# Linear attention and a gated convolution layer on one core: q transposed on TensorE instead of by DMA, the rms factor spread by DMA for two groups instead of three, the convolution on TensorE for one batch instead of two

## The chip, the cores and the metric

The kernel runs on one core of a Trainium2 chip. The core has five engines that each work through their own instructions in order and wait for one another by semaphores: TensorE (PE, matrix products and transposes), VectorE (DVE), ScalarE (ACT), GpSimd (POOL) and SyncE (SP). Sixteen DMA engines move data between HBM and the on-chip memory SBUF. Matrix products land in PSUM, from which DVE or ACT must carry them on.

The metric is the device time of one execution in microseconds. The kernel before takes 247.41 us (median of three runs, 246.47 to 247.62). The execution that the profile shows spans 246.0 us and was timed at 247.78 us. Where an instant is given, it is counted from the start of that span.

## The reference

Eight batches, eight heads, 576 positions, 64 channels per head. First linear attention without softmax with a normalised output, then a layer with a convolution along the sequence as its gate:

```python
kv  = einsum('bhsd,bhse->bhde', k, v)            # 64 x 64 per head
out = einsum('bhsd,bhde->bhse', q, kv)
rms = sqrt(mean(out * out, axis=-1, keepdims=True) + 1e-06)
x   = out / rms * g_norm                         # heads side by side: (8, 576, 512)

h        = maximum(x @ w_in, 0)                  # 512 -> 1024
conv_out = sum of conv_w[k] * h shifted by k-1   # three taps along the sequence
y        = (h * sigmoid(conv_out)) @ w_out       # 1024 -> 512, float32 out
```

q, k, v and the weights come in float32; the DMA casts them to bf16 on the way in.

## The kernel before

The work is cut into five groups of batches, and a table per group says which of two ways is taken for each step. The number after the name of a group below is its place in these tables.

```python
BY_ACT = (1, 1, 1, 0, 0)      # 1/sqrt by ACT (Ln, Exp); 0: by Newton steps on POOL
Q_DMA  = (0, 0, 1, 1, 1)      # q transposed by DMA; 0: by PE
R_DMA  = (0, 0, 1, 1, 1)      # rms factor spread over partitions by DMA; 0: by PE
C_PE   = (1, 1, 0, 0, 0)      # convolution on PE; 0: on DVE
GROUPS = ((0,), (1,), (2, 3), (4, 5), (6, 7))
STEPS  = ((2, 2, 2, 2), (4, 4), (4, 4), (4, 4), (2, 2, 2, 1, 1))
```

Loads go out on POOL's queue, one for each of k, v and q of a batch. Two buffers exist for each name, so a load of batch b waits until the tile of batch b-2 has been read:

```python
loads = pool("loads", 2)
qkv[name, b] = loads.tile([PS, H, R * D], BF16, name=name + "_sb")
nc.gpsimd.dma_start(out=qkv[name, b][:, lo:hi, :], in_=src[b, lo:hi].rearrange(...))
```

q must lie with its channels on the partitions. The two ways (PE works in blocks of 96 positions by 128 channels, six blocks for each of four steps):

```python
if g.by_dma:                                    # Q_DMA
    def tr(...):
        g.qT[bi] = attn.tile([P, H, HS], BF16, name="qT", bufs=QT)
        nc.sync.dma_start_transpose(
            out=g.qT[bi].rearrange("c h (j p) -> c (h j) p", p=PS),
            in_=qkv["q", b].rearrange("p h m -> p (h m)"))
...
if not g.by_dma:
    def tr_mm(...):                             # four times a batch
        ps = one_bank([P, 2, HS], BF16, "qT_ps")
        for i in range(2):
            for j in range(J):
                nc.tensor.transpose(ps[:, i, j * PS:(j + 1) * PS],
                                    q_sb[:, 2 * t + i, j * P:(j + 1) * P], ident[:PS, :PS])
    def tr_out(...):
        move(tst["op"], g.qT[bi][:, 2 * t:2 * t + 2, :], tst["ps"])   # on DVE or ACT
```

For the normalisation, `product` computes `out` into PSUM (`ot_ps`, four small matmuls for a pair of heads), ACT squares it (`sq`), and PE sums the squares (`ss_ps`). ACT or POOL makes 1/sqrt of the sums (`rs`). Then, by R_DMA:

```python
if g.r_dma:                      # out is not kept, but computed a second time
    nc.sync.dma_start(out=scr, in_=g.rs)                   # to DRAM and back,
    for t in range(n_hd):                                  # copied to 64 partitions each
        for i in range(2):
            nc.sync.dma_start(out=g.rb[i * D:(i + 1) * D, t, :, :],
                              in_=row[i:i + 1].to_broadcast([D, 2 * g.G, HS]))
    st["ps"] = product(g, bi, t)                           # out_again
    nc.vector.scalar_tensor_tensor(g.xT[...], st["ps"], g_sb, g.rb[...], mult, mult)
else:                            # out is kept in SBUF (o32, DVE or ACT), rs cut into bf16
    move(ust["op"], g.o32[bi][:, t, :, :], ust["ps"][:, :, :HS], g_sb[:, 0:1])      # keep
    split()                                                # hi, low, mid, rsb on DVE
    nc.tensor.matmul(ps[:, i, :HS], spread[ts, 2 * bi + e, :], g.rsb[ts, :])        # rb_ps
    nc.vector.tensor_mul(g.xT[...], g.o32[bi][...], st["ps"][:, :, :HS])            # x_mul
```

The second half, per group: `h_ps` (eight matmuls for 128 of the 1024 columns and one batch), relu into `h` on ACT or DVE, the convolution, the sigmoid on ACT, the gate on DVE, and `o_ps` (eight matmuls for 128 positions), which ACT or DVE copies to `o_sb` for the store.

```python
if g.c_pe:       # convolution as matmuls with diagonal weights, eight per 128 columns
    nc.tensor.matmul(ps[:, e, off:off + n], diag[:, j, f, :], h[:, src:src + n], ...)    # c_ps
    nc.scalar.activation(cst["c"][...], st["ps"][:, :, :HS], AX.Sigmoid)
else:            # on DVE: two taps per 128 columns, two additions (three pieces) per step
    nc.vector.tensor_scalar_mul(cst["t"][...], g.h[:, f, :], cw_rel[:, j, f:f + 1])      # tap
    nc.vector.tensor_add(c[...], h[...], t[...])                                         # add
    nc.scalar.activation(cst["c"][...], cst["c"][...], AX.Sigmoid, scale=cw_rel[:, 1, f:f + 1])
...
nc.vector.tensor_mul(hs, hs, cst["c"])                                                   # gate
```

None of this is emitted in the order in which it is written. Each step is recorded as an operation with an engine, a cost in microseconds and the operations that it needs; `plan.order()` then plays the list through with these costs, tries 250 variations of the priorities, and emits the best order. Where an operation names two engines, the list also settles which of them does it. The order on each engine is thus fixed when the kernel is built, by costs that are written in the kernel:

```python
t_issue = plan.op("SP", 1.0, tr, deps=[loaded["q", b, h0]] + g.need_qT[bi])
tr_done = plan.op("XBAR", 9.0, None, deps=[t_issue])        # a transpose by DMA
i = plan.op("POOL", 1.3, load, b, name, src, deps=deps)
loaded[name, b, 0] = prev = plan.op("DMA", 3.1, None, deps=[i, prev])   # a load
sp = plan.op("BC", 4.0 + 2.5 * g.G, None, deps=[sc])        # the rms factor by DMA
land = plan.op("OUT", 0.0, None, deps=[so])                 # a store
```

The rings `TWO` (three double banks of PSUM, for `ot_ps`, `rb_ps`, `h_ps`, `c_ps`) and `ONE` (two banks, for `kv_ps`, `qT_ps`, `ss_ps`, `o_ps`) are part of that list too.

Of the kernel before, what the change touches and what calls it, by code (L numbers as in the profile page):

```python
# [54 lines left out]
FP32 = mybir.dt.float32  # L55
# [10 lines left out]
BY_ACT = (1, 1, 1, 0, 0)  # L66
Q_DMA = (0, 0, 1, 1, 1)
R_DMA = (0, 0, 1, 1, 1)
C_PE = (1, 1, 0, 0, 0)
NORM_TABLES = "natural_log_exp_and_others"  # L70
# [32 lines left out]
class Plan:  # L103
# [11 lines left out]
    def op(self, engines, cost, fn, *args, deps=()):  # L115
        engines = engines if isinstance(engines, tuple) else (engines,)
        o = Op(len(self.ops), engines, cost, fn, args, deps)
        o.group = self.group
        self.ops.append(o)
        return o  # L120

    def run(self, places, back=False):
# [13 lines left out]
        while events:  # L136
# [18 lines left out]
            for item in ready:  # L155
                o = ops[item[1]]
                e = next((e for e in o.engines if busy.get(e, 0.0) <= now + 1e-6), None)
                if e is None or not back and any(free[h.ring] < 1 for h in o.takes):
                    continue
                if not back:  # L160
                    for h in o.takes:
                        free[h.ring] -= 1
                end[o.at] = busy[e] = now + o.cost
# [21 lines left out]
    def order(self):  # L185
        ops = self.ops
        way = [0.0] * len(ops)
        for o in reversed(ops):
            way[o.at] = o.cost + self.HOP + max((way[u] for u in o.users), default=0.0)
        best = self.passes([-w for w in way], 8)  # L190
        rnd = random.Random(1)
        for _ in range(self.ROUNDS):
            width = rnd.choice((1, 2, 4, 8))
            each, shift = rnd.random() < 0.7, {}
            places = [e - o.cost + (rnd.gauss(0, width) if each else
                                    shift.setdefault((o.group, o.kind), rnd.gauss(0, width)))
                      for o, e in zip(ops, best[1])]
            got = self.passes(places, 2)
            if got[0] <= best[0]:
                best = got  # L200
        for o, e in zip(ops, best[2]):
            o.engine = e
        return [ops[i] for i in best[3]]


class Group:
    def __init__(self, n, bs, S):
        self.n, self.bs, self.G, self.T = n, bs, len(bs), S * len(bs)
        self.kv, self.qT, self.o32, self.sq = {}, {}, {}, {}
        self.n_o = 0  # L210
# [3 lines left out]
def kernel(  # L214
# [15 lines left out]
    P = 128  # L230
# [132 lines left out]
    def attention(g):  # L363

        first = g.n == 0
        sums = []
        for bi, b in enumerate(g.bs):
            kv_done, free_k, free_q = [], [], []
            hs = H // 2 if first else H
            outs, tr_done, trs, kps = [], None, [], []  # L370
            for h0 in range(0, H, hs):
# [29 lines left out]
                if g.by_dma:  # L401
                    def tr(bi=bi, b=b):
                        g.qT[bi] = attn.tile([P, H, HS], BF16, name="qT", bufs=QT)
                        nc.sync.dma_start_transpose(
                            out=g.qT[bi].rearrange("c h (j p) -> c (h j) p", p=PS),
                            in_=qkv["q", b].rearrange("p h m -> p (h m)"))
                    t_issue = plan.op("SP", 1.0, tr, deps=[loaded["q", b, h0]] + g.need_qT[bi])
                    tr_done = plan.op("XBAR", 9.0, None, deps=[t_issue])
                    free_q.append(tr_done)
                for t in range(h0 // 2, (h0 + hs) // 2):  # L410
                    if not g.by_dma:
# [11 lines left out]
                        def tr_out(bi=bi, t=t, tst=tst):  # L423
# [5 lines left out]
                        tst["op"] = tr_done = plan.op(  # L429
                            ("DVE", "ACT"), 0.5, tr_out, deps=[tmm] + trs[:1])  # L430
                        trs.append(tr_done)
# [85 lines left out]
        if g.r_dma:  # L517
            def scatter():
                scr = dram.tile([P, HS], FP32, name="scr")
                nc.sync.dma_start(out=scr, in_=g.rs)  # L520
                g.rb = big.tile([P, n_hd, 2 * g.G, HS], FP32, name="rb", tag="rb", bufs=O32,
                                padded_shape=[P, n_hd, 4, HS])
# [35 lines left out]
        for bi in range(g.G):  # L558
            for e in range(2):
                for u in range(2):  # L560
# [10 lines left out]
                    def x_mul(bi=bi, e=e, u=u, st=st):  # L571
                        if bi == e == u == 0:
# [4 lines left out]
                            g.xT[:, 2 * u:2 * u + 2, at:at + HS],  # L577
                            g.o32[bi][:, 2 * u:2 * u + 2, e, :], st["ps"][:, :, :HS])

# [6 lines left out]
    def ffn(g):  # L586
# [4 lines left out]
        for nf in STEPS[g.n]:  # L591
# [3 lines left out]
            for f in range(f0, f0 + nf):  # L595
                relu = []
                for bi in range(g.G):
# [12 lines left out]
                    def h_out(f=f, bi=bi, st=st):  # L610
# [111 lines left out]
        for t0 in range(0, g.T, P):  # L722
# [63 lines left out]

    landed = plan.op("CW", 9.0, None)
    mm = plan.op("PE", 0.3, cw_mm, deps=[landed])
# [5 lines left out]

    QT, O32 = 4, 1
    loaded = {}
# [13 lines left out]
    for name in "kvq":  # L810
        loaded[name, 1, 0] = start = plan.op("DMA", 3.1, None, deps=[start])
    w_out_done = plan.op("DMA", 5.5, None, deps=[start])
    prev = w_out_done

    for g in groups:
        g.by_act, g.by_dma, g.r_dma, g.c_pe = (c[g.n] for c in (BY_ACT, Q_DMA, R_DMA, C_PE))
        if g.n > 1:
            for b in g.bs:
                for name, src in (("k", k), ("v", v), ("q", q)):
                    w, wi = where[b - 2]  # L820
                    deps = w.free_q[wi] if name == "q" else w.free_k[wi]
                    i = plan.op("POOL", 1.3, load, b, name, src, deps=deps)
                    loaded[name, b, 0] = prev = plan.op("DMA", 3.1, None, deps=[i, prev])
        def of(attr, b, back, default=()):
# [5 lines left out]
        g.need_kv = {bi: of("free_qT", b, 6) for bi, b in enumerate(g.bs)}  # L830
        g.need_rb = groups[g.n - O32].free_rb if g.n >= O32 else []
        g.need_sq = groups[g.n - 1].free_sq if g.n and g.G + groups[g.n - 1].G > 2 else []
# [38 lines left out]
```

## Time and profile before

| | busy us (share of the 246.0 us) | instructions |
|---|---|---|
| PE, matmul | 185.8 (76%) | 1678 |
| PE, weight load (beside the matmuls) | 112.3 (46%) | 1689 |
| DVE | 129.9 (53%) | 211 |
| ACT | 141.8 (58%) | 224 |
| POOL | 45.6 (19%) | 60 |
| DMA, loads with a cast (POOL's queue) | 43.9% of 16 engines, 16.25 MB | 20960 packets |
| DMA, all issued from SP | 39.2% of 16 engines, 20.52 MB | 26932 packets |

No engine is busy for the whole span, and the shares are averages over stages that have different limits. So the table is read together with the page's rows of 40 equal slices of 6.15 us, which tell when each engine worked, and with the waits. A row of the waits names who was idle, whom it waited for, and for how long in total, how often, and at most. An idle engine costs nothing unless the work that it delays is needed at the end. The DMA engines can have packets of more than one queue under way, so their summed share can be above 1.

### The profile page before, as it was taken

Reading aid. Unit: us, or ns where it says so; the run is one execution under the profiler, and the core shown is the slowest. Engines: PE = TensorE matmul, PEld = TensorE weight load, DVE = VectorE, ACT = ScalarE, POOL = GpSimd, SP = SyncE. Lnnn points to the kernel's source line nnn. Section 1 sums busy time; section 2 is a strip of 40 time slices with the busy share of each in tenths; the row PEclk is TensorE's granted clock in tenths of the full one; section 3 lists DMA queues with packets and bytes.
Section 4 is the critical chain, followed back from the end, with each engine's and each line's share of the span. In section 5 each row is a group of like instructions: output and inputs, shape, how many; then the busy total and the mean of one; then the engine's idle time right before and its main releaser. Section 6 shows DMA issues by size and latency. Waiting matters only on the chain. (4 is left out here: it accounts for less than half of the span.)

```text
span 246.0 us, 4194 instructions
## 1 busy us (share of the span) xinstructions
PE 185.8 (76%) x1678; PEld 112.3 (46%) x1689; DVE 129.9 (53%) x211; ACT 141.8 (58%) x224; POOL 45.6 (19%) x60
## 2 busy tenths in 40 slices
PE   1453987692899308960899969974979999998992
PEld 0331765470375203630276626762534677543440
DVE  2296163641103300311625988999997999976000
ACT  2272479961377406760057794668484889783331
POOL 8740210211121102105700007950000000000000
PEclk9999999998599855995699986997999999999998
DMA  5999999999999999999885930008926030255454
GB/s 78 195 207 203 206 205 203 189 162 166 190 213 224 175 169 207 190 237 227 187 194 140 216 65 0 3 24 188 224 75 173 29 86 2 72 136 160 130 158 114
DMA packets 47911, 37.03 MB, mean 151 GB/s; under 512 B 16252, under 2 KB 43284, under 8 KB 47892
## 3 DMA queue, kind: packets, MB, share of 16 engines
q0 software_dynamic: 20960, 16.25, 43.9%
q1 hardware_dynamic: 26932, 20.52, 39.2%
q8 instruction: 13, 0.21, 0.4%
q14 instruction: 6, 0.05, 0.1%
HBM read 39.60 MB, written 9.88 MB: 201 GB/s over the span
## 5 line engine op out<-in xcount | busy, mean ns | idle before, releaser
L605 PE MATMUL h_ps<-xT,w_in_sb 128*128 128x288 bf16 x512 | 71.8, 302 | 6.7 <-ACT h L616 5.0
L729 PE MATMUL o_ps<-w_out_sb,h 128*128 128x512 bf16 (+1 forms) x285 | 71.0, 400 | 3.5 <-ACT o_sb L344 1.4
L605 PEld LDWEIGHTS <-w_in_sb 128*128 128x128 bf16 x512 | 51.8, 103 | 24.4 <-issue 8.3
L616 ACT ACTIVATE h<-h_ps 128x576 bf16<-128x576 f32 x59 | 37.8, 649 | 24.1 <-PE h_ps L605 23.8
L729 PEld LDWEIGHTS <-h 128*128 128x128 bf16 (+1 forms) x296 | 29.2, 102 | 39.5 <-issue 8.8
L344 ACT ACTIVATE o_sb<-o_ps 128x512 f32<-128x512 f32 (+1 forms) x33 | 19.5, 595 | 38.0 <-PE o_ps L729 36.2
L356 PE MATMUL ot_ps<-qT,kv_sb 64*64 64x288 bf16 x224 | 15.9, 340 | 27.9 <-DMA qT<-q_sb 16.0
L441 ACT ACTIVATE sq<-ot_ps 128x576 bf16<-128x576 f32 x32 | 19.0, 652 | 22.1 <-PE ot_ps L356 20.7
L691 ACT ACTIVATE conv<-conv,cw_rel 128x1152 bf16<-128x1152 bf16 x24 | 28.7, 1251 | 1.7 <-DVE conv L688 1.7
L665 DVE TENSOR_SCALAR tap<-h,cw_rel 128x1152 bf16<-128x1152 bf16 x48 | 24.3, 548 | 8.6 <-ACT h L616 7.8
L696 DVE TENSOR_TENSOR h<-h,conv 128x1152 bf16<-128x1152 bf16 (+2 forms) x15 | 21.4, 1433 | 9.2 <-ACT conv L650 7.6
L544 DVE SCALAR_TENSOR_TENSOR xT<-ot_ps,g_sb,rb 128x576 bf16<-128x576 f32 x24 | 18.3, 811 | 15.0 <-DMA rb<-scr 10.7
L356 PEld LDWEIGHTS <-kv_sb 64*64 64x64 bf16 x224 | 6.5, 113 | 39.0 <-issue 21.1
L688 DVE TENSOR_TENSOR conv<-conv,tap 128x2304 bf16<-128x2304 bf16 (+8 forms) x27 | 18.3, 734 | 0.8
L686 DVE TENSOR_TENSOR conv<-h,tap 128x2304 bf16<-128x2304 bf16 (+8 forms) x27 | 18.2, 729 | 0.3
L618 DVE TENSOR_SCALAR h<-h_ps 128x576 bf16<-128x576 f32 x5 | 3.8, 757 | 25.1 <-PE h_ps L605 25.0
L642 PE MATMUL c_ps<-h,diag 128*128 128x288 bf16 (+2 forms) x128 | 13.7, 256 | 2.9 <-ACT conv L650 2.0
L344 ACT ACTIVATE kv_sb<-kv_ps 64x256 bf16<-64x256 f32 (+1 forms) x28 | 10.1, 362 | 9.1 <-PE kv_ps L381 8.8
L262 POOL DMA_DIRECT2D k_sb<-in_k_dram x9 | 7.0, 775 | 44.7 <-PE kv_ps L381 43.8
L346 DVE COPY o_sb<-o_ps 128x512 f32<-128x512 f32 x4 | 2.8, 691 | 21.9 <-PE o_ps L729 21.9
L642 PEld LDWEIGHTS <-diag 128*128 128x128 bf16 x128 | 11.1, 98 | 5.7 <-issue 3.2
L262 POOL DMA_DIRECT2D q_sb<-in_q_dram x9 | 6.7, 749 | 32.1 <-DMA qT<-q_sb 26.2
(60 smaller groups left out, 121.5 us busy)
## 6 DMA issues: line engine op xcount, KB each, us to landing
rb<-scr SPq DMA_DIRECT2D x24, 288.0 KB, 7.3
out_dram<-o_sb SPq DMA_DIRECT2D x24, 192.0 KB, 2.5
k_sb<-in_k_dram POOLq DMA_DIRECT2D x7, 576.0 KB, 14.4
v_sb<-in_v_dram POOLq DMA_DIRECT2D x7, 576.0 KB, 17.1
q_sb<-in_q_dram POOLq DMA_DIRECT2D x7, 576.0 KB, 13.6
out_dram<-o_sb SPq DMA_DIRECT2D x24, 128.0 KB, 2.4
out_dram<-o_sb SPq DMA_DIRECT2D x24, 64.0 KB, 2.0
w_in_sb<-in_moe_w_in_dram POOLq DMA_DIRECT2D x2, 512.0 KB, 11.7
```

The lines of the kernel that those rows point to most:

```text
L344: nc.scalar.activation(dst, src, AX.Copy, scale=1.0 if scale is None else scale)
L356: nc.tensor.matmul(ps[i * D:(i + 1) * D, e, :HS], g.kv[bi][es, t, i, :], g.qT[bi][es, 2 * t + i, :], start=True, stop=True)
L441: nc.scalar.activation(g.sq[bi, t], ust["ps"][:, :, :HS], AX.Square)
L544: nc.vector.scalar_tensor_tensor(g.xT[:, t, bi * S:(bi + 1) * S].rearrange("p (e n) -> p e n", n=HS), st["ps"][:, :, :HS], g_sb[:, 0:1], g ...
L605: nc.tensor.matmul(ps[:, e, :HS], w_in_sb[:, t, f * P:(f + 1) * P], g.xT[:, t, at:at + HS], start=(t == 0), stop=(t == n_hd - 1))
L616: nc.scalar.activation(dst, st["ps"][:, :, :HS], AX.Relu)
L642: nc.tensor.matmul(ps[:, e, off:off + n], diag[:, j, f, :], h[:, src:src + n], start=m < 2, stop=m >= len(todo) - 2)
L665: nc.vector.tensor_scalar_mul(cst["t"][:, f - f0, :], g.h[:, f, :], cw_rel[:, j, f:f + 1])
L688: nc.vector.tensor_add(c[:, :, there], c[:, :, there], t[:, :, here])
L691: nc.scalar.activation(cst["c"][:, f - f0, :], cst["c"][:, f - f0, :], AX.Sigmoid, scale=cw_rel[:, 1, f:f + 1])
L696: nc.vector.tensor_mul(hs, hs, cst["c"])
L729: nc.tensor.matmul(st["ps"][:n, :], g.h[:, f, t0:t0 + n], w_out_sb[:, f, :], start=(f == 0), stop=(f == n_ff - 1))
```

## The change

Three entries in the tables move. q is transposed by PE for all batches, so the six DMA transposes go. The rms factor is spread by DMA for batches 4 to 7 only; batches 2 and 3 take the way over PE, where `out` is kept in SBUF. The convolution of batch 1 moves from PE to DVE. Since PE now transposes more, it hands over a part of its convolution.

The other edits concern the model behind the order. Transfers that used to have resources of their own (`XBAR`, `BC`, `OUT`) now occupy the one resource `DMA` that the loads occupy too, followed by a `LAND` delay that occupies nothing. Operations that can go to DVE or ACT get a cost for each of the two. Costs of loads and issues are set lower. The kept `out` of a group becomes one tile for both its batches.

```diff
-Q_DMA = (0, 0, 1, 1, 1)
-R_DMA = (0, 0, 1, 1, 1)
-C_PE = (1, 1, 0, 0, 0)
+Q_DMA = (0, 0, 0, 0, 0)
+R_DMA = (0, 0, 0, 1, 1)
+C_PE = (1, 0, 0, 0, 0)
...
+        cost = cost if isinstance(cost, tuple) else (cost,) * len(engines)
...
-                e = next((e for e in o.engines if busy.get(e, 0.0) <= now + 1e-6), None)
+                e = next((e for e in o.engines
+                          if e == "LAND" or busy.get(e, 0.0) <= now + 1e-6), None)
...
-                    tr_done = plan.op("XBAR", 9.0, None, deps=[t_issue])
+                    tr_done = plan.op("DMA", 4.5, None, deps=[t_issue])
+                    tr_done = plan.op("LAND", 3.0, None, deps=[tr_done])
...
-                            ("DVE", "ACT"), 0.5, tr_out, deps=[tmm] + trs[:1])
+                            ("DVE", "ACT"), (0.46, 0.65), tr_out, deps=[tmm] + trs[:1])
...
-                        if t == 0:
-                            g.o32[bi] = big.tile([P, n_hd, 2, HS], FP32, name="o32", tag="rb", bufs=O32,
-                                                 padded_shape=[P, n_hd, 4, HS])
-                        dst, src = g.o32[bi][:, t, :, :], ust["ps"][:, :, :HS]
+                        if bi == t == 0:
+                            g.o32 = big.tile([P, 2 * g.G, n_hd, HS], FP32, name="o32", tag="rb",
+                                             bufs=1, padded_shape=[P, 4, n_hd, HS])
+                        dst = g.o32[:, 2 * bi:2 * bi + 2, t, :]
+                        src = ust["ps"][:, :, :HS]
...
-                    ust["op"] = kp = plan.op(("DVE", "ACT"), 0.7, keep, deps=[om] + kps[:1])
+                    ust["op"] = kp = plan.op(("DVE", "ACT"), (0.81, 0.75), keep, deps=[om] + kps[:1])
...
-            sp = plan.op("BC", 4.0 + 2.5 * g.G, None, deps=[sc])
+            sp = plan.op("DMA", 3.0 * g.G, None, deps=[sc])
+            sp = plan.op("LAND", 2.5, None, deps=[sp])
...
-                    st["op"] = hr = plan.op(EITHER, 0.7, h_out,
+                    st["op"] = hr = plan.op(EITHER, (0.66, 0.77), h_out,
...
-            st["op"] = ev = plan.op(EITHER, 0.65, o_out, deps=[om])
+            st["op"] = ev = plan.op(EITHER, (0.6, 0.69), o_out, deps=[om])
             so = plan.op("SP", 0.5, o_store, deps=[ev])
-            land = plan.op("OUT", 0.0, None, deps=[so])
+            land = plan.op("DMA", 0.65, None, deps=[so])
+            land = plan.op("LAND", 2.0, None, deps=[land])
...
-                    i = plan.op("POOL", 1.3, load, b, name, src, deps=deps)
-                    loaded[name, b, 0] = prev = plan.op("DMA", 3.1, None, deps=[i, prev])
+                    i = plan.op("POOL", 0.9, load, b, name, src, deps=deps)
+                    loaded[name, b, 0] = prev = plan.op("DMA", 2.95, None, deps=[i, prev])
```

More of the change, by code (lines that the diff above doesn't have):

```diff
@@ L162, in run @@
                         free[h.ring] -= 1
-                end[o.at] = busy[e] = now + o.cost
+                end[o.at] = busy[e] = now + o.cost[o.engines.index(e)]
                 eng[o.at] = e
@@ L188, in order @@
         for o in reversed(ops):
-            way[o.at] = o.cost + self.HOP + max((way[u] for u in o.users), default=0.0)
+            way[o.at] = min(o.cost) + self.HOP + max((way[u] for u in o.users), default=0.0)
         best = self.passes([-w for w in way], 8)
@@ L194, in order @@
             each, shift = rnd.random() < 0.7, {}
-            places = [e - o.cost + (rnd.gauss(0, width) if each else
+            places = [e - min(o.cost) + (rnd.gauss(0, width) if each else
                                     shift.setdefault((o.group, o.kind), rnd.gauss(0, width)))
@@ L208, in __init__ @@
         self.n, self.bs, self.G, self.T = n, bs, len(bs), S * len(bs)
-        self.kv, self.qT, self.o32, self.sq = {}, {}, {}, {}
+        self.kv, self.qT, self.sq = {}, {}, {}
         self.n_o = 0
@@ L365, in attention @@
         first = g.n == 0
-        sums = []
+        sums, kps = [], []
         for bi, b in enumerate(g.bs):
@@ L369, in attention @@
             hs = H // 2 if first else H
-            outs, tr_done, trs, kps = [], None, [], []
+            outs, tr_done, trs = [], None, []
             for h0 in range(0, H, hs):
@@ L520, in scatter @@
                 nc.sync.dma_start(out=scr, in_=g.rs)
-                g.rb = big.tile([P, n_hd, 2 * g.G, HS], FP32, name="rb", tag="rb", bufs=O32,
+                g.rb = big.tile([P, n_hd, 2 * g.G, HS], FP32, name="rb", tag="rb", bufs=1,
                                 padded_shape=[P, n_hd, 4, HS])
@@ L577, in x_mul @@
                             g.xT[:, 2 * u:2 * u + 2, at:at + HS],
-                            g.o32[bi][:, 2 * u:2 * u + 2, e, :], st["ps"][:, :, :HS])
+                            g.o32[:, 2 * bi + e, 2 * u:2 * u + 2, :], st["ps"][:, :, :HS])
                     rb = plan.op("PE", 0.24, rb_mm, deps=[sp] + g.need_xT)
@@ L785, in cw_ratio @@
             nc.vector.tensor_mul(cw_rel[:, j, :], cw[:, j, :], sgn[:, 1, :])
-    landed = plan.op("CW", 9.0, None)
+    landed = plan.op("LAND", 9.0, None)
     mm = plan.op("PE", 0.3, cw_mm, deps=[landed])
@@ L792 @@
     ratio_done = plan.op("DVE", 1.2, cw_ratio, deps=[cw_done])
-    QT, O32 = 4, 1
+    QT = 4
     loaded = {}
@@ L810 @@
     for name in "kvq":
-        loaded[name, 1, 0] = start = plan.op("DMA", 3.1, None, deps=[start])
+        loaded[name, 1, 0] = start = plan.op("DMA", 2.95, None, deps=[start])
     w_out_done = plan.op("DMA", 5.5, None, deps=[start])
@@ L830 @@
         g.need_kv = {bi: of("free_qT", b, 6) for bi, b in enumerate(g.bs)}
-        g.need_rb = groups[g.n - O32].free_rb if g.n >= O32 else []
+        g.need_rb = groups[g.n - 1].free_rb if g.n else []
         g.need_sq = groups[g.n - 1].free_sq if g.n and g.G + groups[g.n - 1].G > 2 else []
```

## The prediction

> **What bounds the kernel now.** I read the 40 slices first, since the shares of the whole span hide the stages.
>
> ```profile
> PE   1453987692899308960899969974979999998992
> DVE  2296163641103300311625988999997999976000
> ...
> PEclk9999999998599855995699986997999999999998
> DMA  5999999999999999999885930008926030255454
> ```
>
> Each digit is 6.15 us. DMA is full up to slice 19 (about 123 us) while DVE is nearly idle and PE has holes; after that DMA is light, and DVE and PE are full. There are two regimes with an edge near 124 us. The PE timeline fits: the first product `h_ps` of group 2 starts at 123.91 us. I cut the span there and at 24.5 us, where group 0 has its `xT`, and asked for the stretches.
>
> ```profile
> 24.50:124.00 99.50, 69.33 (x843) 42.77 (x846) 28.14 (x42) 52.97 (x90) 19.54 (x27) 0.85 1.24 196
> 124.00:228.00 104.00, 93.52 (x654) 57.60 (x659) 88.62 (x130) 74.93 (x110) 14.26 (x12) 0.95 0.44 106
> 183.40:241.40 58.00, 56.49 (x322) 30.56 (x327) 38.52 (x65) 36.65 (x55) 0.00 (x0) 1.00 0.39 105
> ```
>
> The columns are the stretch, its length, busy time of PE, PE's weight loads, DVE, ACT and POOL, then the granted clock, DMA's share and GB/s. In the middle stretch DVE works 28 of 99.5 us, ACT 53, and PE 69 at a clock of 0.85. Nothing is full but DMA. In the last, PE is full at full clock. What the middle waits for, from the waits of 24 to 124 us:
>
> ```profile
> POOL k_sb L262 <- PE kv_ps L381: 42.2, 5, 11.3
> POOL q_sb L262 <- DMA qT<-q_sb: 26.2, 4, 12.1
> ...
> PEld L356 <- DMA qT<-q_sb: 17.3, 3, 11.1
> PE ot_ps L356 <- DMA qT<-q_sb: 16.0, 2, 10.8
> ```
>
> This is a ring. The load of q waits (26.2 us) until a DMA transpose has emptied its buffer. PE waits for the same transposes before `ot_ps`, and standing there in order it comes late to the next `kv_ps`, so the loads of k wait for PE (42.2 us). Why the transposes are slow, from the DMA queues of 82 to 92.7 us, a stretch in which PE does nothing:
>
> ```profile
> q1 hardware_dynamic: 2378, 0.93, 68.9%
> q0 software_dynamic: 1243, 0.93, 64.1%
> ...
> qT<-q_sb SPq DMA_TRANSPOSE x2, 14.6
> ```
>
> q1 carries transposes and two stores here, q0 the loads. They halve the engines: the loads move 0.93 MB in 10.7 us (87 GB/s), against 2.90 MB in 14.3 us (203 GB/s) in 28 to 42.3 us, where they are alone. A transpose takes 14.6 us to land, where the kernel's model assumes 9. The idle time also costs clock:
>
> ```profile
> 92.67 0.45 PE L356 MATMUL ot_ps<-qT,kv_sb 64*64 64x288 bf16 x4 [10.82 <-DMA qT<-q_sb]
> 93.05 3.62 PE L729 MATMUL o_ps<-w_out_sb,h 128*64 128x512 bf16 x8
> ...
> 104.69 1.90 PE L729 MATMUL o_ps<-w_out_sb,h 128*128 128x512 bf16 x8
> ```
>
> Eight `o_ps` take 3.62 us after the pause, and 1.90 later.
>
> **What the Trainium skill says.** "DMA: Bandwidth & Descriptors", section "Issuing engines are not separate DMA queues": DMAs of every issuer run on the same 16 engines and interleave. The trace agrees (203 against 87 GB/s above), so both queues belong in one model, as the change has it. "TensorE: Matmul & The Clock Gate", section "Part 1: The HAM clock gate (the "warmup" mystery)": an idle TensorE falls to half its clock until it has been busy for a window. It agrees: clock 0.56 in 92.7 to 98.4 us, 1.00 after. The same page, "Part 4: PE-mode transpose", says transposes don't count as busy for that gate; no stretch here shows that apart, and I keep it as a risk. "SBUF — State Buffer", section "SBUF: two separate sides": GpSimd and DVE's two-port modes exclude each other at a shared port. The trace fits: during the Newton steps on POOL at 153 us the three first additions of a step take 3.87 us, and 2.70 elsewhere.
>
> **The change, part by part.** I take effective times out of full bursts: `h_ps` 0.99 us per eight matmuls (13 times eight in 12.90), `o_ps` 1.73 (the cadence of its copies in the tail), `c_ps` 0.83, `kv_ps` 0.93, `ot_ps` 0.26 per four, `rb_ps` 0.24 per pair, `ss_ps` 0.34. For the moved transposes and their copies:
>
> ```profile
> L419 PE MATMUL qT_ps<-ident,q_sb 96*128 96x96 bf16 x48 | 4.0, 241 | 2.7 <-DMA q_sb<-in_q_dram 1.9 <-ACT qT L344 0.7
> L344 ACT ACTIVATE qT<-qT_ps 128x576 bf16<-128x576 bf16 x4 | 2.6, 649 | 1.4 <-PE qT_ps L419 1.4
> L346 DVE COPY qT<-qT_ps 128x576 bf16<-128x576 bf16 x4 | 1.8, 458 | 6.7 <-PE qT_ps L419 6.7
> ```
>
> Six transposes overlap to about 0.31 us.
>
> *Removed:* six DMA transposes (3.5 MB twice through the engines, 14.6 us each); eight of 24 `rb` transfers (2.3 MB); eight second products (2.1 us of PE) and eight `xT` with `rb` (8 x 0.811 = 6.5 us of DVE); half of the convolution on PE (8 x 0.83 = 6.6 us).
>
> *Added:* PE: 24 x 0.31 = 7.4 us of transposes and 8 x 0.24 = 1.9 us of `rb_ps`. PE's sum is unchanged: 7.4 + 1.9 - 2.1 - 6.6 = +0.6 us. DVE, by counts in the changed order: 16 more `qT` copies (7.3), 7 more relus (5.3), 5 more kept `out` (4.1), one split (1.7), eight `xT` from `rb_ps` (6.0), 16 taps of half length (5.0), additions in two steps (6.7), less 6.5 above and 1.9 for copies that go to ACT: +27.7, so about 158 us. ACT: eight `qT` (5.2), three kept (2.2), four `kv_sb` (1.1), less seven relus (4.5), and the sigmoids the same: about +5, so 147.
>
> No engine gains work that must make the span longer: 158 us on DVE is far under 246. The gain must come from the middle stretch. So I summed the changed order between the same marks, the first `h_ps` of group 0 and that of group 2.
>
> | PE | before | after |
> |---|---|---|
> | middle | kv 6, qT 0, ot 24, ss 4, c 16, h 16, o 9, rb 0: 57.9 | kv 4, qT 16, ot 16, ss 4, rb 8, c 8, h 16, o 5: 47.3 |
> | last | ot 24, ss 2, h 48, o 28: 102.9 | kv 2, qT 8, ot 24, ss 2, h 48, o 32: 114.1 |
>
> The middle took 100.2 us (23.7 to 123.9) for 57.9. Afterwards DVE has 50.5 us in it against 28 (by counts in its order times the times of back-to-back runs of each group: 8 relus 5.8, 15 `qT` 6.9, 8 kept `out` 6.2, two splits 3.5, 12 `xT` 8.5, 16 taps 5.0, additions 6.5, gates 5.6, the rest 2.5), and ACT 51.6 (20 squares 11.4, 16 sigmoids 9.6, seven table loads 9.0, 16 `kv_sb` 6.2, 8 relus 5.0, the rest 10.4), beside PE's 47.3. DMA no longer holds it. Loads alone take 0.59 MB / 203 GB/s = 2.9 us each; batch 2 was in at 42.3 us (when its transpose could be issued), so batch 3 is in at 51 and batch 7 at about 86. Group 2 needs batch 3 only: products to about 65 us, ln and exp with their two table loads 3.5 us, then 13 us of DVE's order up to the `xT` that the first `h_ps` needs: 81.5 as the earliest. Three engines with 47 to 52 us each, in fixed orders and waiting for one another, will not all be full; PE managed 88% in 28 to 42.3 us (12.52 of 14.3), where only it and ACT were loaded. At 82% of DVE's 50.5 the middle ends at 24.5 + 61.5 = 86 us, 38 us sooner.
>
> The last stretch had PE at 102.9 in 117.5 us (123.9 to 241.4). DVE set it: it ended at 227.2, and the last `o_ps` took 14.3. Afterwards DVE has 92.5 us of work there (48 taps 22.1, additions 37.0, gates 15.6, 16 `xT` 12.0, the rest 5.8); at 93% busy, with 3 to start and 14.3 after, PE ends 117 us on. PE's own sum is 114.1 and loses some 10 (cold clock and small waits; it lost 14.6 before): 124 us. PE is the longer. The end of the last `o_ps` comes at 86 + 124 = 210, plus 4.6 for copy, store and end (241.4 to 246.0) = 214.6, plus 1.4 from span to time (246.0 to 247.4) = **216 us**, 13% less.
>
> **Rivals.** *DVE becomes the bound throughout.* It goes from 130 to 158 us and has no slack in the middle. For it: it was 88.6 of 104 us busy in 124 to 228. If its Newton collision comes twice, some 4 us each, and it reaches only 75% in the middle: the end of the middle is at 92, the span at 222, the time near 224. *The transposes were hidden anyway,* and the loads, at about 203 GB/s, set the middle. Against it: the loads would be through at 86 us, and the trace shows PE idle for 10.82 us on one transpose. Were it so, the group would start near 110, and the time would be about 238. *The rms factor of groups 3 and 4 arrives too late:* once the middle is short, Newton (9.3 to 15 us) and transfers (about 10) take a larger part of the way to `xT`. In the changed order DVE reaches those `xT` about 23 and 50 us after the mark, which just suffices; being late costs 5 to 8 us. *Better than reckoned:* if the planned order holds at 95%, the middle ends at 78, PE is warm, and the time is near 206.
>
> **Range and chances.** Start of group 2's `h_ps` 80 to 94 us, the rest 119 to 130: 8 in 10 within 206 to 228. Slower than 242 would need the middle to stay above 110 us. Faster by over 2%: 0.95, within 2%: 0.03, slower: 0.02.
>
> **What would show it.** In the changed profile: DMA's full slices end near 90 us with q0 alone; waits of POOL's loads for PE shrink from 42 us; the first `h_ps` of group 2 stands between 80 and 94 us; DVE is busy for 155 to 162 us, ACT for 145 to 150; the middle's clock rises from 0.85 to 0.95 or more. I am wrong if that start lies past 100, if DVE's taps are slowed by POOL for more than 8 us, or if PE waits for `qT` copies on DVE or ACT as long as it waited for the DMA.

## The result and the profile after

The changed kernel takes 218.17 us (median of four runs, 217.68 to 220.53) against 246.94 us for the kernel before beside it (246.34 to 247.62). The ratio is 0.885, with a 95% interval of 0.878 to 0.892. The prediction was 216 us, in a range of 206 to 228. The profiled execution took 217.68 us; its span is 215.6 us, at a mean clock of 0.971.

The 40 slices of the changed kernel, each 5.39 us, in the rows that were shown of before:

```profile
PE   1363898969999697997999999498899999997991
...
DVE  2096527688789769867988699999969899972000
...
PEclk9999999999999759999999999889999999999997
DMA  4999999999999999122994108911552101554553
```

The full slices of DMA end with the sixteenth, at 86 us, where they ended near 123. DVE showed digits of 0 to 6 in the middle of the kernel before; here it shows 6 to 9 from the seventh slice to the thirty-sixth. PE's holes down to 0 and 3 in that stretch are gone. The product `h_ps` of group 2, whose start is the edge between the two stages, stands in PE's timeline (start, length, instruction) at 87.70 us; it stood at 123.91. The second line is the last eight `o_ps`:

```profile
87.70 5.07 PE L610 MATMUL h_ps<-xT,w_in_sb 128*128 128x288 bf16 x40
...
196.93 14.20 PE L734 MATMUL o_ps<-w_out_sb,h 128*128 128x512 bf16 x64 [1.16 <-DVE h L701]
```

So 36.2 us were gained before the edge. From the edge to the end of the span it took 122.1 us before (246.0 - 123.9) and takes 127.9 us now (215.6 - 87.7): 5.8 us are given back there. The stretches of the changed kernel, in the columns of the prediction (stretch, length, PE, weight loads, DVE, ACT, POOL, clock, DMA's share, GB/s):

```profile
23.30:87.70 64.40, 57.30 (x734) 37.13 (x736) 47.01 (x90) 51.10 (x86) 13.00 (x17) 0.95 1.28 206
87.70:137.00 49.30, 45.69 (x488) 31.12 (x489) 40.82 (x57) 36.73 (x59) 18.21 (x23) 1.00 0.50 119
137.00:196.90 59.90, 56.23 (x338) 31.44 (x342) 53.29 (x85) 43.09 (x63) 0.00 (x0) 0.97 0.36 92
```

The middle is 64 us long instead of 100, PE is busy for 89% of it (57.30 of 64.40) at a clock of 0.95, and the loads still stream at 206 GB/s. The two stretches behind the edge keep PE at 93 to 94% and DVE at 83 to 89%. What POOL's loads wait for in the middle and, in the last row, PE for a load, from the waits of 23.3 to 87.7 us of the changed kernel (who, for whom; total us, times, longest):

```profile
POOL q_sb L264 <- PE qT_ps L422: 18.6, 4, 8.6
POOL k_sb L264 <- PE kv_ps L383: 18.0, 3, 9.4
...
POOL k_sb L264 <- PE ot_ps L358: 5.0, 1, 5.0
POOL q_sb L264 <- PE ot_ps L358: 4.8, 1, 4.8
...
PE kv_ps L383 <- DMA v_sb<-in_v_dram: 0.5, 1, 0.5
```

The waits for DMA transposes are gone with the transposes. The loads of k wait for `kv_ps` 18 us instead of 42, but the loads of q now wait for the transposes on PE. The four rows of POOL make 46 us, where the two of before made 68 (42.2 and 26.2). They only say that a buffer is free late. What they cost is seen where an engine then waits for a load, and in this stretch PE's products did so for 0.5 us in all (the last row).

### The profile page after: what moved, and what is told of

Read it like the earlier page. It is cut to its first block, busy times and chain, and to the rows that moved or that the text cites. A ratio compares the mean times of both kernels' runs of the same rounds, so it can differ in the third digit from the quotient of the medians.

```text
span 215.6 us, 4371 instructions
## 1 busy us (share of the span) xinstructions
PE 182.1 (84%) x1742; PEld 111.4 (52%) x1753; DVE 153.2 (71%) x266; ACT 145.5 (68%) x235; POOL 43.1 (20%) x60
## 5 line engine op out<-in xcount | busy, mean ns | idle before, releaser
L610 PEld LDWEIGHTS <-w_in_sb 128*128 128x128 bf16 x512 | 50.4, 101 | 20.9 <-issue 5.6
L621 ACT ACTIVATE h<-h_ps 128x576 bf16<-128x576 f32 x52 | 33.3, 649 | 23.7 <-PE h_ps L610 23.3
L696 ACT ACTIVATE conv<-conv,cw_rel 128x1152 bf16<-128x1152 bf16 (+1 forms) x32 | 34.4, 1128 | 0.2
L670 DVE TENSOR_SCALAR tap<-h,cw_rel 128x1152 bf16<-128x1152 bf16 (+1 forms) x64 | 29.4, 495 | 5.7 <-ACT h L621 4.6
L691 DVE TENSOR_TENSOR conv<-h,tap 128x1152 bf16<-128x1152 bf16 (+8 forms) x33 | 20.8, 683 | 0.3
L693 DVE TENSOR_TENSOR conv<-conv,tap 128x1152 bf16<-128x1152 bf16 (+8 forms) x33 | 20.1, 665 | 1.0
L422 PE MATMUL qT_ps<-ident,q_sb 96*128 96x96 bf16 x192 | 13.8, 222 | 4.3 <-ACT kv_sb L346 2.3
L348 DVE COPY qT<-qT_ps 128x576 bf16<-128x576 bf16 x20 | 8.8, 454 | 10.9 <-PE qT_ps L422 10.8
L358 PE MATMUL ot_ps<-qT,kv_sb 64*64 64x288 bf16 x192 | 14.2, 318 | 1.9 <-ACT sq L444 0.9
L549 DVE SCALAR_TENSOR_TENSOR xT<-ot_ps,g_sb,rb 128x576 bf16<-128x576 f32 x16 | 12.8, 813 | 4.0 <-PE ot_ps L358 3.8
L422 PEld LDWEIGHTS <-q_sb 96*128 96x128 bf16 x192 | 10.9, 106 | 7.1 <-issue 3.1
L581 DVE TENSOR_TENSOR xT<-o,rb_ps 128x576 bf16<-128x576 f32 x16 | 11.2, 747 | 2.6 <-PE rb_ps L573 2.6
L383 PE MATMUL kv_ps<-v_sb,k_sb 96*64 96x64 bf16 x384 | 8.9, 208 | 4.3 <-DMA v_sb<-in_v_dram 4.3
```

The lines of the kernel that those rows point to most:

```text
L358: nc.tensor.matmul(ps[i * D:(i + 1) * D, e, :HS], g.kv[bi][es, t, i, :], g.qT[bi][es, 2 * t + i, :], start=True, stop=True)
L422: nc.tensor.transpose(ps[:, i, j * PS:(j + 1) * PS], q_sb[:, 2 * t + i, j * P:(j + 1) * P], ident[:PS, :PS])
L610: nc.tensor.matmul(ps[:, e, :HS], w_in_sb[:, t, f * P:(f + 1) * P], g.xT[:, t, at:at + HS], start=(t == 0), stop=(t == n_hd - 1))
L621: nc.scalar.activation(dst, st["ps"][:, :, :HS], AX.Relu)
L670: nc.vector.tensor_scalar_mul(cst["t"][:, f - f0, :], g.h[:, f, :], cw_rel[:, j, f:f + 1])
L691: nc.vector.tensor_add(c[:, :, here], h[:, :, here], t[:, :, there])
```

## The experiments

Each kernel is the changed one with the edit that is shown, unless the kernel before is named. Ratios are to the kernel before, run beside it; a difference "in us" is the difference of two ratios times 247 us. T0 is the start of the first `h_ps` of group 2, read in the profiled execution. The theory is that of the prediction: the transposes held the middle. A kernel whose tables or costs differ gets an order of its own, so such a difference holds the part and the order that came with it. Some executions were disturbed and are left out of the times below, which leaves two where q goes by DMA with the old costs (for the version with stores from ACT, the profiled execution, of 939 us, is one of those left out) and one for the rms factor without v (whose profile is of an execution of 233.9 us that is left out).

**Undo the transposes alone** (changed kernel, q of batches 2 to 7 by DMA again):

```diff
-Q_DMA = (0, 0, 0, 0, 0)
+Q_DMA = (0, 0, 1, 1, 1)
```

> The kernel after, with q of batches 2 to 7 transposed by DMA again (Q_DMA = 0,0,1,1,1) and all else as changed. My theory, that the transposes by DMA take the shared DMA engines from the loads and so stretch the middle stage, expects most of the gain to go: group 2's first h_ps at 100 to 115 us instead of 87.7, the time 232 to 242 us. The rival, that the new order (a model in which DMA traffic counts) carries the gain whatever the way of q, expects 217 to 225 us.

Measured: 253.1 and 256.7 us, ratio 1.036 [1.025, 1.048], T0 103.8 us. That is 37 us more than the changed kernel, and more than the kernel before. The load of q waits for the transposes again (waits of this kernel):

```profile
POOL q_sb L264 <- DMA qT<-q_sb: 38.9, 4, 13.0
```

A transpose took 16.6 us to land (median of six), while the order had been made for 1 + 4.5 + 3. This is too much of a loss for one part. It was not clear how much of it belongs to the transposes and how much to an order made for transposes that are faster than the real ones.

**The same, with costs nearer to the traces in the order's model.**

```diff
-t_issue = plan.op("SP", 1.0, tr, ...)
-tr_done = plan.op("DMA", 4.5, None, deps=[t_issue])
-tr_done = plan.op("LAND", 3.0, None, deps=[tr_done])
+t_issue = plan.op("SP", 8.0, tr, ...)
+tr_done = plan.op("DMA", 9.0, None, deps=[t_issue])
+tr_done = plan.op("LAND", 5.0, None, deps=[tr_done])
```

> The run with q transposed by DMA in the changed kernel (256.8 us), planned anew with costs of a transpose near what the traces show (SP 8, DMA 9, landing 5 us instead of 1, 4.5, 3). If most of that run's loss against the kernel before comes from an order made for transposes that are twice as quick as real ones, 238 to 248 us. If the transposes themselves cost it, 252 us or more.

Measured: 236.5 us, ratio 0.960 [0.953, 0.967], T0 111.6 us. Of the 37 us, half (0.076 of the ratio, 19 us) was the order. The other half (0.075, 18.5 us) stays with an order made for slow transposes (22 us planned from issue to use; here they landed 12.5 us after their issue in the median, 19.4 at most), and is put down to the transposes here. The two halves lie in different places. With the wrong costs it took 151.1 us from T0 to the end of the span, with the better ones 124.4 (127.9 in the changed kernel): what the order lost was lost behind the edge, and what the transposes cost lies ahead of it. PE still stands for one load behind them, in its timeline:

```profile
102.69 1.49 PE L383 MATMUL kv_ps<-v_sb,k_sb 96*64 96x64 bf16 x48 [11.55 <-DMA v_sb<-in_v_dram]
```

**Transposes by DMA, stores issued from ACT.** SP issues both the transposes and the stores of the output, so a store could stand behind a transpose.

```diff
-nc.sync.dma_start(      # store of o_sb
+nc.scalar.dma_start(
```

> The run with q transposed by DMA in the changed kernel (256.8 us), with its output stores issued from ACT instead of SP. In its trace SP is taken by three transposes from 85.6 to 112.4 us, and ACT waits 8.3 us in one go for a store to free its buffer, and PE for ACT. If transposes also cost by standing ahead of the stores in SP's queue, 236 to 250 us. If only the transfers themselves and the waits for them cost, 253 us or more.

Measured: 253.6 and 256.0 us, ratio 1.033 [1.023, 1.043], which is the ratio of the kernel with SP's stores (1.036). That stores stand behind transposes in SP's queue is not what costs.

**The new model with the old tables.**

```diff
-Q_DMA, R_DMA, C_PE = (0, 0, 0, 0, 0), (0, 0, 0, 1, 1), (1, 0, 0, 0, 0)
+Q_DMA, R_DMA, C_PE = (0, 0, 1, 1, 1), (0, 0, 1, 1, 1), (1, 1, 0, 0, 0)
```

> All three tables as in the kernel before, with the changed model of the order. My theory expects the model alone to do little, since DMA still has the same work: 238 to 247 us. The rival, that the order carries the gain, expects 218 to 230 us.

Measured: 250.9 us, ratio 1.020 [1.014, 1.026], T0 110.8 us. With the old ways the new model loses 5 us; the theory had expected no loss. The edge comes 13 us earlier than in the kernel before, but the rest of the span takes 139.2 us instead of 122.1. The model counts 8.5 us from the issue of a transpose to its landing (the old one 10), and here it took 15.6; loads of q waited 52.9 us for it. That this is the reason is likely after the run with better costs, but was not tested here.

**The new tables with the old model** (all costs and resources of the model set back):

```diff
-tr_done = plan.op("DMA", 4.5, ...); plan.op("LAND", 3.0, ...)
+tr_done = plan.op("XBAR", 9.0, ...)
-... (0.46, 0.65) ... (0.81, 0.75) ... (0.66, 0.77) ... (0.6, 0.69)
+... 0.5 ... 0.7 ... 0.7 ... 0.65
-sp = plan.op("DMA", 3.0 * g.G, ...); plan.op("LAND", 2.5, ...)
+sp = plan.op("BC", 4.0 + 2.5 * g.G, ...)
... (stores and loads likewise)
```

> The three tables of the kernel after, with the costs and the separate transfer resources of the kernel before (the kept out stays one tile for a group). My theory, that the tables carry the gain, expects 217 to 224 us. The rival, that the tables need the changed model to pay, expects 228 us or more.

Measured: 224.6 us, ratio 0.910 [0.903, 0.918], T0 92.3 us. The edits of the model bring 6 us with the new tables. So most of the gain is in the tables: the same model gains 6 us with the new ones and loses 5 with the old ones.

**Fewer loads: v of batches 2 to 7 is not loaded**, and k's tile is read in its place, so a third of these loads (3.5 MB) is left out. It was done to both kernels.

```diff
+if name == "v" and b > 1:
+    qkv["v", b] = qkv["k", b]
+    return
```

On the kernel before:

> The kernel before, in its own order, with v of batches 2 to 7 not loaded (the tile of k is read in its place, so kv is k times k there): six of 24 loads, 3.5 MB, leave the DMA queue. If loads and transposes hold one another up on the shared engines, the middle shrinks by the time of the six loads and more: 222 to 232 us, and a transpose lands well under 14.6 us. If the transposes are slow by themselves, or their chain of issue is, the time stays at 240 to 247 us and they land in 12 us or more.

Measured: 235.8 us, ratio 0.960 [0.953, 0.966], T0 114.3 us. A transpose landed in 9.0 us instead of 14.6. This lies between the two expectations: leaving out six loads is worth about 10 us, their own transfers included, and T0 is still 27 us later than in the changed kernel. Contention with the loads is a part of the cost, not the whole.

On the changed kernel:

> The kernel after, in its own order, with v of batches 2 to 7 not loaded (the tile of k is read in its place). The DMA row of the changed profile is full up to 86 us and group 2's first h_ps stands at 87.7. My theory, that the loads are no longer awaited in the middle and PE, DVE and ACT together set it, expects that h_ps at 85 to 88 us and 215 to 219 us. The rival, that the loads still set the middle, expects h_ps at 80 us or before and 207 to 212 us.

Measured: 217.6 us, ratio 0.885 [0.880, 0.891]; nothing changed. DMA's row and the start of `h_ps`, from the page and PE's timeline of this kernel:

```profile
DMA  4999999989992991022994109911552101554553
```

```profile
87.64 5.07 PE L613 MATMUL h_ps<-xT,w_in_sb 128*128 128x288 bf16 x40
```

DMA now has slices at 2 and 1 before the edge, and the edge stands at 87.64 us, where it stood at 87.70. So what the loads move does not set the middle of the changed kernel. POOL's waits for free buffers are still there in this run (40.5 us for k and q up to the edge), so it doesn't take them away.

**Undo the rms factor alone** (batches 2 and 3 by DMA again):

```diff
-R_DMA = (0, 0, 0, 1, 1)
+R_DMA = (0, 0, 1, 1, 1)
```

> The kernel after with the rms factor of group 2 spread by DMA again (R_DMA = 0,0,1,1,1). My theory, that from rs to xT the way over DRAM costs the middle some 8 to 15 us of waiting, part of which other work fills, expects 221 to 228 us. The rival, that the 8 us of DVE work saved in the middle count for more, expects 210 to 217 us.

Measured: 236.0 us, ratio 0.957 [0.949, 0.965], T0 95.5 us: 18 us lost, more than either expectation. Three views of this kernel show the first half of it. SP's queue (issue of `scr`, then of the eight `rb`), after ACT has `rs` at 66.5 us:

```profile
66.50 0.38 SPq L524 DMA_DIRECT2D scr<-rs  x1
71.94 7.12 SPq L530 DMA_DIRECT2D rb<-scr  x8
```

DVE's timeline, with what it was idle for in brackets:

```profile
81.64 0.82 DVE L549 SCALAR_TENSOR_TENSOR xT<-ot_ps,g_sb,rb 128x576 bf16<-128x576 f32 x1 [2.66 <-DMA rb<-scr]
85.76 0.82 DVE L549 SCALAR_TENSOR_TENSOR xT<-ot_ps,g_sb,rb 128x576 bf16<-128x576 f32 x1 [3.30 <-DMA rb<-scr]
89.99 0.82 DVE L549 SCALAR_TENSOR_TENSOR xT<-ot_ps,g_sb,rb 128x576 bf16<-128x576 f32 x1 [3.42 <-DMA rb<-scr]
93.92 2.99 DVE L549 SCALAR_TENSOR_TENSOR xT<-ot_ps,g_sb,rb 128x576 bf16<-128x576 f32 x4 [3.12 <-DMA rb<-scr]
```

And the stretches, in the columns from above:

```profile
84.00:90.00 6.00, 0.32 (x4) 0.11 (x4) 0.83 (x2) 2.16 (x4) 0.00 (x0) 0.78 1.23 235
```

Every 4 us one pair of `rb` lands, and DVE does one `xT`. For these six microseconds PE works 0.32 and DVE 0.83, and DMA runs at 235 GB/s. PE has as much work in the middle as in the changed kernel (57.5 us), but the middle is 72.2 us long, not 64.4. The other 12 us are lost behind the edge (235.7 - 95.5 = 140.2 us against 127.9). The clock of 95.5 to 150 us is 0.82, and SP waits 14.4 us at a stretch for the factor that POOL computes for another group, with stores behind it in its queue; ACT waits 6.0 us for such a store, and PE 5.7 us for ACT. These stand one behind the other in the trace, but no run took them apart. Nor was this kernel planned anew with better costs, as the one with transposes was: its order counts 11.5 us from the issue of `scr` to the last `rb` (3.0 + 6.0 + 2.5), and in the trace the last `xT` that waits starts 27 us after that issue. So how much of the 18 us belongs to the order stays open.

**The same without v of batches 2 to 7**, to ask whether the loads slow the `rb`:

> The run with the rms factor of group 2 spread by DMA in the changed kernel (236.0 us), in the same order, with v of batches 2 to 7 not loaded (the tile of k is read in its place). In that run DVE waited 12.5 us in four goes for the transfers of the factor while loads were under way. If the transfers are late because the loads share their engines, these waits fall under 6 us and the time to 222 to 230 us. If the way over DRAM is slow by itself, or the loss is elsewhere, 232 us or more.

Measured: 227.7 us, once, so no ratio is formed. The time lies in the range of the first expectation, the waits in the profile do not: the `xT` still wait 11.3 us for `rb` (12.5 with v), a pair landing every 4 us as before, with DMA full. So it is not borne out that the loads of v make this wait, and where the 8 us went that one execution gained is open. The loads of q and k still run beside the transfers. In the changed kernel eight of them, for group 3, run with only stores beside them. They are issued from 99.75 us on and land between 103.8 and 113.4 us, one every 1.4 us (0.29 MB each, some 215 GB/s), where with loads beside them it was one every 2 us. So the eight fill the engines for about 11 us even without loads.

**Undo the convolution alone** (batch 1 on PE again):

```diff
-C_PE = (1, 0, 0, 0, 0)
+C_PE = (1, 1, 0, 0, 0)
```

> The kernel after with the convolution of batch 1 on PE again (C_PE = 1,1,0,0,0): DVE loses 11.7 us of work, PE gains 6.6. If, as I read the stages, PE sets the last stage and all three engines the middle, the two cancel: 216 to 221 us. If DVE sets the middle, 209 to 214 us.

Measured: 220.8 us, ratio 0.894 [0.888, 0.900], T0 90.0 us, about 2 us more than the changed kernel, with intervals that overlap. The middle of this kernel:

```profile
23.30:89.95 66.65, 58.72 (x812) 40.40 (x812) 37.92 (x64) 48.18 (x82) 11.51 (x15) 0.95 1.26 204
```

DVE has 9 us less to do here than in the changed kernel (37.92 against 47.01), and the middle is 2 us longer. PE is again busy for 88% of it. The time lies in the range of the first expectation: DVE's work does not set the middle.

**Less `o_ps`: two of eight matmuls left out in groups 2 and 3.** It takes 7.8 us of work from PE in the last stretch and nothing from DVE.

```diff
-for f in range(n_ff):
+last = n_ff - 1 if g.n in (0, 1, 4) else n_ff - 3
+for f in range(last + 1):
```

> The kernel after, in its own order, with two of the eight matmuls of each o_ps of groups 2 and 3 left out (18 x 2 x 0.216 = 7.8 us of PE work in the last stage, none of it in the tail; the output of batches 2 to 5 lacks their part). If PE sets the last stage, as I reckoned, the time falls by 4 to 8 us, to 210 to 214 us. If DVE sets it, the time stays at 216 to 219 us.

Measured: 214.8 us, ratio 0.874 [0.867, 0.881], 3 us less by the ratios (the intervals overlap), between the two expectations. In the profiled execution T0 is 2 us later than in the changed kernel, for which no cause was found, and from T0 to the end of the span it takes 122.9 us against 127.9. So 5 of the 7.8 us come through in that stretch. Where the rest stays (stretches of this kernel):

```profile
136.00:193.90 57.90, 49.78 (x310) 28.38 (x312) 55.68 (x88) 45.76 (x65) 0.00 (x0) 0.97 0.42 106
```

PE goes down to 86% of the stretch and DVE up to 96%, where it was 94% and 89%. DVE is the next bound, only a few microseconds behind.

**A try at a better version: 1/sqrt of group 2 on POOL**, which takes two changes of ACT's tables and the logarithm and exponential from ACT.

```diff
-BY_ACT = (1, 1, 1, 0, 0)
+BY_ACT = (1, 1, 0, 0, 0)
```

> A try at a better version: the kernel after with 1/sqrt of group 2 by Newton steps on POOL instead of Ln and Exp on ACT (BY_ACT = 1,1,0,0,0). ACT loses two table loads (2.6 us) and two more passes in the middle, which three engines share; the way from ss to rs grows by some 9 us, which other work has to fill. If the middle is set by the sum of work, 212 to 216 us; if by the chain from ss to xT, 219 to 226 us.

Measured: 223.0 us, ratio 0.906 [0.900, 0.912], T0 95.4 us: 5 us slower, in the range of the second expectation, that the chain from `ss` to `xT` sets the middle. The factor is ready at 79.06 us instead of 70.15, 8.9 us later, and T0 is 7.7 us later. The Newton steps take POOL from 69.2 to 79.0 us; the next load of q is issued only then. DVE's additions in that time are slower (DVE's timeline of this kernel):

```profile
70.88 2.73 DVE L691 TENSOR_TENSOR conv<-h,tap 128x1152 bf16<-128x1152 bf16 x3
...
77.56 2.19 DVE L693 TENSOR_TENSOR conv<-conv,tap 128x1152 bf16<-128x1152 bf16 x3
```

The same three additions take 1.50 us where POOL rests. So this try does not beat the changed kernel.

## Why the prediction was right, and where its working was not

**The middle ends at 86 us: it ended at 87.7.** The mechanism that carried this step is real, and is part of what the runs show. The transposes cost 18.5 us with an order made for slow ones, and taking a third of the loads from the kernel before made a transpose land in 9.0 us instead of 14.6 and brought 10 us. But the prediction put the whole gain of the middle down to this ring, and named the `rb` of group 2 only as 2.3 MB that go. In the trace of before the way of the rms factor takes the other part. ACT has the factor of group 2 at 82.8 us; then, in SP's queue of the kernel before:

```profile
86.88 8.30 SPq L404 DMA_TRANSPOSE qT<-q_sb  x1
95.28 0.53 SPq L520 DMA_DIRECT2D scr<-rs  x1
101.22 6.64 SPq L526 DMA_DIRECT2D rb<-scr  x8
```

SP had four stores and a transpose ahead of it, sent the factor out 12 us after it was ready, and the last `xT` started at 123.5 us, 41 us after it. In the changed kernel ACT has it at 70.15 us and the last `xT` starts at 88.0, 18 us later. The instant at which the factor of group 2 is ready cuts the way to the edge in two (us, each in the profiled execution):

| kernel | factor ready | T0 | from factor to T0 |
|---|---|---|---|
| before | 82.8 | 123.9 | 41.1 |
| changed | 70.15 | 87.7 | 17.6 |
| changed, transposes by DMA | 82.9 | 103.8 | 20.9 |
| the same, better costs | 85.1 | 111.6 | 26.5 |
| changed, rms factor of group 2 by DMA | 66.5 | 95.5 | 29.0 |

Of the 36.2 us, 12.7 were gained ahead of the factor and 23.5 behind it. Undoing the transposes brings back the first part, with the factor ready at 82.9 us or later, and adds 3 to 9 us to the second. Undoing the rms factor makes the second part 11.4 us longer. The other 12 us of the second part are those for which the factor of the kernel before stood in SP's queue, most of them behind the transpose (82.8 to 95.28 us; with the rms factor undone in the changed kernel it went out at once, at 66.50). Each of these kernels has an order of its own, so this is a reading of traces that fits and not a sum that has to come out. The term was there to be read: in the trace of before, `xT` of group 2 waits 10.7 us for `rb`. The prediction asked this question only for groups 3 and 4.

**The parts do not add up, and the sum was right for another reason.** Undoing one part costs 37 us (18.5 with better costs), 18, 2 and, for the model, 6; even with the smaller number that is 45 us against 29 measured. The costs of wrong orders are in these numbers too (of the 37 us, half), and no run tells how much two orders differ by chance. The estimate of 86 us did not rest on such a sum. It was built from what the engines still have to do in the changed order once no transfer holds them, and so took in the rms factor and the model without naming them. No number was given for the edits of the model.

**DVE at 82% paces the middle: the wrong engine.** The length came out (64.4 us against 61.5), in part by luck: DVE had 47.0 us of work and not 50.5, filled 73% of the stretch and not 82%, and taking 9 us from it gained nothing. PE is the fullest, at 89%. PE's 47.3 us in the prediction's table were too few by 10. The table lacked the attention of batch 1, before and after: the trace has 5 `kv_ps`, 20 `qT_ps` and `ot_ps`, 5 `ss_ps` and 12 `rb_ps` where the table has 4, 16, 4 and 8. At the prediction's own times that is 0.93 + 1.24 + 1.04 + 0.34 + 0.96 = 4.5 us. The times out of full bursts were too short as well. In PE's timeline of the changed kernel:

```profile
38.97 0.91 PE L647 MATMUL c_ps<-h,diag 128*128 128x288 bf16 x8
39.72 1.14 PE L610 MATMUL h_ps<-xT,w_in_sb 128*128 128x288 bf16 x8
40.80 0.95 PE L383 MATMUL kv_ps<-v_sb,k_sb 96*64 96x64 bf16 x48
```

Eight `h_ps` between other products take 1.14 us, not the 0.99 of a burst (16 times 0.15 is 2.4 us), and the `o_ps` of this stretch took 10.9 us for the 8.7 reckoned, at a mean of 427 ns. That makes 56.4 of the 57.3 us. It does not follow that PE sets the middle. Cut at the factor, the middle of the changed kernel falls in two (stretches in the columns from above):

```profile
23.30:70.15 46.85, 43.33 (x626) 30.77 (x627) 33.00 (x61) 36.20 (x61) 8.88 (x12) 1.00 1.30 209
70.15:87.70 17.55, 13.97 (x118) 6.36 (x113) 14.01 (x29) 14.90 (x26) 4.11 (x6) 0.81 1.22 199
```

Ahead of the factor PE is busy for 92% at full clock. Behind it no engine is above 85%. What runs there is the chain from the factor over the split and `rb_ps` to the `xT`, for which the prediction had 13 us (68.5 to 81.5) as the least and which took 17.6. The run with Newton steps fits: there T0 moved with the factor. With the convolution of batch 1 on PE it was otherwise: the factor was ready at 68.5 us, and PE worked on `h_ps` of group 1 up to the edge. No run took work from PE in the middle, so what PE's work alone sets there is not shown.

**The last stretch takes 124 us: it took 123.4** (87.7 to 211.1). PE's busy time there is 101.9 + 14.2 = 116.1 us, for a predicted 114.1, and 7.3 us are lost where 10 were put. "PE is the longer" holds by a few microseconds only: DVE ends its last gate at 196.9 and PE's last eight `o_ps` wait for it, and with 7.8 us less on PE, 5 come through. DVE's 92.5 us were 94.1.

**The small terms.** Copy, store and end took 4.5 us for 4.6, and from span to time 2.1 us for 1.4. ACT (145.5 us) and the clock of the middle (0.95) are where they were to be. The risk kept for the clock is not settled: it stood at 0.50 from 73.2 to 80.0 us, just behind the factor, after pauses of PE of 0.73 and 1.03 us between small products and transposes, and no run shows which of them did it. DVE's 153.2 us lie just under the 155 to 162, since its work in the middle was 47.0 us and not 50.5. The waits of k's loads for PE shrank from 42 us to 18, but the waits of q's loads that came in their place were not foreseen; they cost next to nothing in the middle, where PE's products waited 0.5 us for a load.

**The rivals.** That the loads set the middle is refuted: with 3.5 MB of them gone the edge did not move. That DVE bounds throughout is refuted for the middle and nearly true for the end; the Newton steps slowed it less than feared there: the three first additions at 124.6 us took 3.40 us against 2.70, where they had taken 3.87 before. The late rms factor of group 3 did not occur, but by little: its last `rb` landed at 113.4 us and DVE reached that `xT` at 114.60.

## What to carry to other kernels

Where loads fill the DMA engines, a transfer that stands in the chain of dependences (a transpose, a broadcast by way of DRAM) can cost more than its own length, as both did here: it waits for its queue, shares the DMA engines, and leaves other engines idle behind it; look for each such chain from its producer to its last consumer, not only for the longest wait. An order that is made from a cost model is only as good as the durations of its transfers: with a transpose planned at 8.5 us from issue to use instead of 22, the same tables lost 19 us more. To predict a change of several parts, sum what each engine has left to do and ask how full it can get, in times taken from mixed stretches rather than bursts; the costs of undoing the parts one by one did not add up to the gain. A mean share over a stage can hide that its end is a chain: cut the stage at the instants that the chain passes.

## What the runs showed of the hardware that was not expected

- A DMA transpose of 96 x 3072 bf16 (0.59 MB) inside SBUF took 14.6 us to land beside full loads, 9.0 us with a third of the loads gone (medians of six), and it held SP's queue for 3.0 to 10.1 us in the kernel before.
- Broadcasts of 288 KB from DRAM to 64 partitions landed one every 1.4 us with only stores beside them, and one every 2 us beside loads (an estimate from the first and the last landing: 103.8 and 113.4 us in the changed kernel, 79.3 and 93.8 with the factor of group 2 by DMA).
- Three additions of 1152 bf16 columns on DVE take 2.2 to 2.7 us beside POOL's Newton steps, and 1.5 us alone; a tap of 576 columns 0.80 us, and 0.37 alone.
